# Block 2's half rows by mirrored gathers and scatters instead of TensorE flips, with a new issue order

## The chip, the cores and the metric

The kernel runs on one core of a Trainium2 chip. The metric is the device time of one execution in microseconds (us). Each engine takes its instructions in the order in which the program issues them: PE (TensorE), DVE (VectorE), ACT (ScalarE), POOL (GpSimd), and SP, which here only issues DMAs. Lines such as L617 are lines of the kernel's source.

## The reference

The inputs are `q`, `k`, `v` (2048 rows S of 640 columns D, bf16), a short filter `shift_k` (640 x 4), a long filter `ssm_k` (640 x 2048), a vector `ssm_D`, and three matrices of a SwiGLU feed-forward network (FFN) with 1728 inner columns. Cut to what matters, the reference computes:

```
k_shift[t] = sum over i = 0..3 of k[t-i] * shift_k[:, i]      (causal, per column)
kv  = k_shift * v
y   = causal convolution of kv with ssm_k along the 2048 rows (by FFT) + kv * ssm_D
h   = q + layernorm(q) * y
g   = layernorm(h)
out = h + (silu(g @ w_gate) * (g @ w_up)) @ w_down
```

## The kernel before

**Blocks and tiles.** The 2048 rows are four blocks n = 0..3 of 512; a block is four tiles q = 0..3 of 128 rows, one row to a partition. The long convolution is done by blocks: every block of `kv` and of the filter is taken to a spectrum of 512 values with constant matrices (`WX` for the rows, `WG` for the filter, `WI` back), spectra are multiplied and added over pairs of blocks, and the sum is taken back.

**Half rows and their mirror images.** The basis is symmetric, so the way back needs half of the work: `inverse` (L587) makes, for each half m = 0, 1, an even part `es` and an odd part `os`, 128 rows each (PE L597, copied from PSUM by ACT L601). Their sum is rows of tile 2+m in natural order; their difference is rows of tile 1-m in mirrored order (last row first). Tiles 0 and 1 of a block thus come out mirrored. The letter of the block in `HOW` (L101) says what is done about it:

- `J`: the block's rows are loaded in natural order by one DMA of SP (L274). The difference is turned by PE: four matmuls with the flip matrix (L617) of `es` and `os` into a PSUM buffer of pool A, which DVE multiplies by the normalized rows (L620). Then DVE adds each tile to its rows (L610 and L622).
- `G`: SP loads tiles 2 and 3 only. Tiles 0 and 1 are fetched mirrored, by two indirect DMAs of POOL (`load_x`, L577) with a constant table of row numbers (`mirror`). DVE forms the difference with L608, as it forms the sum, and handles the natural and the mirrored tile together by L626 (multiply) and L627 (add), 128 x 1280 each. The two tiles stay mirrored through the FFN, row by row, and their results are written back by indirect DMAs of POOL (`down`, L752), where `J` uses a plain store of SP.

With `HOW = 'GGJJ'`, blocks 0 and 1 go by gathers and scatters, blocks 2 and 3 by flips:

```python
if half == 0 or HOW[n] != "J":
    add("DVE", ..., (TA, TS)[half](y[:, 1 - half, :], es[m][:], os_[m][:]))       # L608
else:
    nc.tensor.matmul(ps(g)[:, h, 0:NH], flip[part], (es, os_)[part][m][...], ...)  # L617
    add("DVE", ..., TM(r3(y[:, 1 - half, :]), ps(g)[:, :, 0:NH], r3(xln[...])))    # L620
```

**The other stages.** `g_transform` (L344 on PE, L346 on ACT) makes a filter block's spectrum from the transposed filter: block 0's is transposed by PE (L314), blocks 1 to 3 by a transposing DMA of SP (L304). `front` makes `kv` of a block: for block 0 DVE multiplies rows with the short filter (L383) and PE shifts and adds them (L393), turning tiles 0 and 1 (V: L401, ACT L403, DVE L404/L406); for later blocks DVE does all of it (L361, L366, L367, L368) and PE turns two tiles (L418). L421 and L422 fold the block into its even and odd halves. `x_transform` is L433 on PE and L438 on ACT. `pair` is DVE's spectral products and sums (L443, 128 x 2560). `ln` takes sums over rows on ACT (L527, L530, L531), `root` the inverse square root on POOL (L550), `scale` the normalized rows on DVE (L563) or ACT (L559, L560). SP transposes normalized rows for the FFN (L648). `ffn` is L685 on PE (two groups of five matmuls for each of 14 column chunks, U), `sg` (L690) and `uc` (L697) on ACT, and their product `tT` (L699) on DVE; then the down projection on PE (L733 adds the residual, L736), `o` on ACT (L745) or DVE (L747), and the store. The last tile ends with L714 and L719.

**Openings for POOL.** `port` (L537) is a small DVE reduction (128 x 96) that a POOL instruction is made to wait for. Every scatter (L752) and most roots (L550) have one; the gathers (L577) have none. For some roots a one-column DVE copy of the result follows (L552).

**Buffers.** PSUM has two pools of two buffers, A (transforms, inverses, flips) and F (filter transforms, FFN). `es`, `os`, `hl`, `sg`, `uc`, `ot`, `wg`, `wu`, `k4`, `vt`, the rows `x` and the transposed rows `hT` have two buffers each. Block 2's rows use the buffer of block 0's, so they can be fetched once block 0's down projection has read them.

**The order.** All instructions are first collected in a list of 1017 entries (`Plan.add`), an entry being some matmuls of one PSUM group, one DVE instruction, one DMA and so on. They are then issued in the order of `SEQUENCE` (L105), a constant permutation of the entries' numbers; nothing else orders them, beyond the waits for data and buffers that each one carries:

```python
def order(self):
    assert sorted(SEQUENCE) == list(range(len(self.ops)))
...
with tc.manual_schedule():
    for i in seq:
        plan.ops[i]["fn"]()
```

Of the kernel before, what the change touches and what calls it, by code (L numbers as in the profile page):

```python
# [97 lines left out]
VEC = (0,)  # L98
SPAN = 96
TURN = ()  # L100
HOW = 'GGJJ'  # L101
BACK = "SSSS"
TRANS = {1: 0, 2: 0, 3: 0}
WARM = (0.43, 5, 0)
SEQUENCE = [int(i) for i in """  # L105
2 19 20 5 0 8 10 7 1 3 24 21 22 34 72 69 4 11 13 12 14 17 15 73 16 25 18 27 26 28 6 31 61 71 29 23 30 56 53 54 51 62 32 76 33 74 229 58 63 52 77 64 57
75 55 78 65 206 59 198 80 60 207 228 79 35 89 66 199 70 43 67 36 81 68 37 208 90 38 98 91 82 209 39 99 85 83 210 44 92 86 40 100 230 93 88 233 45 101
234 94 200 102 46 41 95 103 96 201 42 47 97 202 104 106 48 148 105 203 49 211 149 214 109 221 150 315 50 220 116 314 108 156 215 151 204 157 107 172
205 158 173 111 212 159 190 216 213 174 231 110 118 114 191 222 175 112 115 152 217 113 223 160 153 218 237 117 132 224 119 219 130 133 225 434 120
327 161 164 326 226 131 433 121 442 182 165 441 227 176 183 137 123 134 184 177 135 122 248 136 192 249 138 185 256 124 139 193 250 257 166 125 140  # L110
186 141 167 251 194 128 187 126 129 142 443 154 195 232 127 162 87 143 435 155 252 235 196 180 163 253 258 146 168 197 436 147 259 444 254 238 144 178
181 145 169 260 179 170 245 261 255 188 171 243 236 262 316 437 263 242 189 317 9 438 321 244 318 322 338 319 246 323 439 339 333 324 320 239 247 328
334 325 330 350 445 335 264 329 336 345 265 331 351 449 340 332 266 341 342 362 346 446 343 337 268 347 352 363 348 344 353 267 357 349 269 358 359
354 272 355 270 375 360 401 440 369 402 374 240 271 455 370 361 274 429 371 273 364 372 356 275 430 365 278 387 386 276 277 293 399 279 456 373 366
450 451 295 367 388 398 381 400 296 280 452 382 299 281 294 447 394 457 383 384 297 376 368 385 431 395 377 396 284 453 389 300 378 432 379 390 285
380 403 458 391 392 298 404 448 397 301 282 405 393 283 302 459 406 305 478 410 306 286 411 460 407 477 303 412 304 454 408 413 287 461 423 291 307
409 462 289 292 475 489 414 497 424 290 84 308 498 476 490 499 559 415 491 677 479 500 417 312 416 481 501 313 310 418 480 492 311 419 483 560 420 571
493 421 572 425 482 494 502 426 484 495 463 503 561 485 504 427 562 496 487 563 566 564 486 567 568 583 565 578 569 584 505 669 464 579 570 488 580
573 581 574 507 575 465 590 596 506 595 576 591 468 577 469 509 585 466 586 607 582 510 467 513 608 428 592 508 536 593 514 602 587 594 511 588 470
603 471 589 597 512 537 598 604 472 671 599 515 600 620 619 605 288 473 679 614 670 516 422 521 678 522 712 517 615 606 538 523 616 617 518 609 544  # L120
601 519 672 539 610 631 611 520 632 711 626 525 633 612 627 526 618 613 680 621 628 524 629 713 622 540 623 634 541 527 681 715 635 624 528 639 625
673 636 630 545 637 682 640 529 692 542 650 641 546 691 530 814 543 651 547 548 642 638 549 652 674 714 685 686 532 653 675 550 717 643 533 551 693
644 813 654 801 802 534 645 552 694 535 646 655 553 695 657 716 647 676 658 555 687 556 683 663 648 656 684 688 557 696 664 689 554 649 690 558 474
697 665 698 659 719 733 741 718 734 666 735 667 720 660 736 803 699 742 721 661 804 805 737 723 806 808 738 722 809 810 825 743 725 811 826 739 700
815 701 807 812 727 816 817 820 818 724 744 821 702 837 819 726 822 832 838 823 703 833 824 728 706 827 740 729 828 834 849 835 731 829 745 850 830
844 704 831 845 836 746 749 705 839 730 846 840 847 861 841 751 851 842 862 707 747 843 856 848 748 732 853 852 873 708 874 750 857 662 854 858 863
241 709 752 859 868 753 869 860 754 757 870 761 864 755 758 871 779 910 765 875 756 881 780 855 759 872 865 309 866 781 760 867 531 882 762 766 883
763 876 782 884 764 783 877 784 769 785 788 770 786 922 710 891 767 668 878 768 879 892 773 787 775 880 893 771 776 789 772 885 790 909 791 894 774
792 886 777 778 895 887 795 793 921 797 794 888 798 903 889 796 904 890 799 896 800 897 898 899 900 905 901 906 916 907 917 918 911 919 920 912 913
933 908 923 914 934 915 924 925 928 926 927 929 930 945 935 931 946 932 936 937 940 938 939 941 942 957 952 943 958 902 944 953 954 947 955 956 948  # L130
949 969 964 950 970 951 959 960 961 982 981 965 962 966 976 967 983 968 977 963 978 989 979 980 971 990 991 972 973 984 974 975 985 992 986 993 987
988 994 995 996 999 997 1000 998 1001 1002 1005 1003 1006 1004 1007 1008 1011 1009 1014 1012 1013 1010 1015 1016
""".split()]


def dve(n, psum=False):
    return (120 + n) / 960 if psum else 0.06 + n / 1920
# [7 lines left out]
def kernel(  # L145
# [107 lines left out]
    def r3(a):  # L253
        return a.rearrange("p (a b) -> p a b", a=2)

    def ps(group):
        return ps_of[group[0]][plan.held[group]]
# [241 lines left out]
    def ln(n, q, which, pr, t0=0.0):  # L499
# [12 lines left out]
        else:  # L512
            j = q % 2
            if which == 1 and HOW[n] == "X" and q < 2:
                g = ("A", "M", n, q)
# [38 lines left out]
    def scale(dst, n, q, which, key, pr):  # L554
        s, src, c = sm[n, q, which], xin[n % 2][:, q, :], column(n, q, which)
        vec, r = which == 2 and n in VEC, rstd[:, c:c + 1]

        def on_act():
            nc.scalar.activation(s[:, 2:3], s[:, 0:1], ACT.Copy, scale=r)  # L559
            nc.scalar.activation(dst, src, ACT.Identity, scale=r, bias=s[:, 2:3])  # L560

        def on_dve():
            nc.vector.tensor_scalar(dst, src, s[:, 0:1], r, op0=ALU.subtract if vec else ALU.add, op1=ALU.mult)  # L563
        on = (n, which) in XACT and not vec
        add(*(("ACT", act(D) + 0.22, on_act) if on else ("DVE", 0.355, on_dve)), r=[f"sm{n}{q}{which}", f"x{n % 2}_{q}"], w=[key], pr=pr)
# [5 lines left out]
    @stage  # L571
    def load_x(n, pr, queue="SP"):
        if HOW[n] == "G":
            x = xin[n % 2]
            load(queue, x[:, 2:4, :], xq[n * MB + 256:(n + 1) * MB, :].rearrange("(m p) d -> p m d", p=P), [f"x{n % 2}_{q}" for q in (2, 3)], pr, 320, t0=(14, 30, 0, 0)[n])
            for q in (1, 0):
                add("POOL", 2.5, lambda q=q: nc.gpsimd.indirect_dma_start(out=x[:, q, :], out_offset=None, in_=xq[:, :], in_offset=mirror(n, q), bounds_check=S_TOT - 1,  # L577
                                                                      oob_is_err=False), r=["idx"], w=[f"x{n % 2}_{q}"], pr=pr, kb=160, t0=(14, 30, 0, 0)[n])
        else:
            load(queue, xin[n % 2][:], xq[n * MB:(n + 1) * MB, :].rearrange("(m p) d -> p m d", p=P), [f"x{n % 2}_{q}" for q in range(4)], pr, 640, t0=(14, 30, 0, 0)[n])  # L580
        for q in range(4):
            ln(n, q, 1, pr + 30, t0=(26, 50, 0, 0)[n])
        for qs in ((2, 1), (3, 0)) if n == 0 else ((0, 1, 2, 3),):
            root(n, qs, 1, pr + 30)

    @stage
    def inverse(n, pr):  # L587
        a, ak = A[n], Ak[n]
        x, b = xin[n % 2], n % 2
        for m in range(2):  # L590
# [13 lines left out]
            for half, q in pairs:  # L604
                yk, lk, xk = keys[q]
                scale(xln[:, 1 - half, :], n, q, 1, lk, pr)
                if half == 0 or HOW[n] != "J":
                    add("DVE", dve(D), lambda m=m, half=half: (TA, TS)[half](y[:, 1 - half, :], es[m][:], os_[m][:]), r=[f"eo0{m}", f"eo1{m}"], w=[yk], pr=pr)  # L608
                    if HOW[n] == "J":
                        add("DVE", dve(D), lambda half=half: TM(y[:, 1 - half, :], y[:, 1 - half, :], xln[:, 1 - half, :]), r=[lk], w=[yk], pr=pr)  # L610
                else:
# [8 lines left out]
                    add("DVE", dve(D, True), lambda g=g, half=half: TM(r3(y[:, 1 - half, :]), ps(g)[:, :, 0:NH], r3(xln[:, 1 - half, :])), r=[g, lk], w=[yk], pr=pr, rel=("A", g))  # L620
                if HOW[n] == "J":
                    add("DVE", dve(D), lambda q=q, half=half: TA(x[:, q, :], x[:, q, :], y[:, 1 - half, :]), r=[yk], w=[xk], pr=pr)  # L622
            if HOW[n] != "J":
                lo, step = 1 - m, 1 + 2 * m
# [213 lines left out]
```

## Time and profile before

| | us |
|---|---|
| median of 6 runs (lowest, highest) | 285.39 (284.8, 286.09) |
| the profiled execution | 285.3 |
| its span, from first to last instruction | 283.5 |
| PE busy | 272.9 (96%) |
| DVE busy | 218.4 (77%) |
| ACT busy | 207.4 (73%) |
| POOL busy | 36.1 (13%) |

The granted TensorE clock is 1.000. The slices of the profile cut the span in 40 parts of 7.09 us; a digit is the busy share of a slice in tenths, 9 being 90% or more. A line of the chain or the timeline gives the start, the duration, the engine and the source line; in the timeline `out<-in` follows, then the shape, how many instructions were put together (x4), and in brackets how long the engine was idle before and what ended that. SPq is the DMA-issuing queue of SP. Durations on POOL are rough.

### The profile page before, as it was taken

To read this page: it belongs to the slowest core of one execution; us is meant where nothing else is said; L and a number is where in the kernel's file an instruction comes from. 1 tells how busy PE (TensorE), PEld (TensorE's weight loads), DVE (VectorE), ACT (ScalarE), POOL (GpSimd) and SP (SyncE) were. 2 spreads that over 40 slices of the span, in tenths; PEclk is the share of its full clock that TensorE was granted. 3 is DMA by queue.
4 is the path that set the end of the run, shared out by engine and by line. 5 is a ranking of instruction groups with operands and counts; after the bars stand their busy time and mean duration, and the time that the engine had idled before them with its cause. 6 is when DMAs were issued, how large, how long until landed. Compare 5 with 4: busy or idle time off the path is not lost.

```text
span 283.5 us, 4423 instructions
## 1 busy us (share of the span) xinstructions
PE 272.9 (96%) x1639; PEld 160.6 (57%) x1639; DVE 218.4 (77%) x295; ACT 207.4 (73%) x408; POOL 36.1 (13%) x30
## 2 busy tenths in 40 slices
PE   6699999999999999989999999999999999999995
PEld 1467777776444547654455477644455765444673
DVE  1659999999999999999999999999997510211212
ACT  4698898899654999956999997689859945546300
POOL 3203000111800005600030102100300110000000
PEclk9999999999999999999999999999999999999999
DMA  5999991822475870499837099535522561664011
GB/s 169 327 293 319 201 315 27 299 49 46 103 233 136 263 252 1 104 221 250 247 93 205 20 295 217 139 95 152 139 57 71 140 144 29 200 165 116 0 49 46
DMA packets 69466, 44.13 MB, mean 156 GB/s; under 512 B 28290, under 2 KB 67267, under 8 KB 69316
## 3 DMA queue, kind: packets, MB, share of 16 engines
q1 hardware_dynamic: 68914, 42.33, 55.7%
q0 software_dynamic: 384, 1.31, 1.4%
q8 instruction: 13, 0.21, 0.3%
q10 hardware_dynamic: 146, 0.20, 0.2%
q14 instruction: 9, 0.07, 0.1%
HBM read 36.63 MB, written 2.62 MB: 138 GB/s over the span
## 4 chain that ended last, share of the span: by engine, by line
DVE 35%; PE 26%; ACT 8%; issue 3%; DMA 2%; DVEq 0%; ACTq 0%
DVE s L443 14%; PE psF L685 14%; PE psF L736 9%; DVE T L443 9%; DVE tT L699 3%; DMA hT<-hl 2%; DVE k L361 2%; ACT junk L530 2%; PE psF L714 1%; ACT junk L527 1%; ACT sg L690 1%; ACT uc L697 1%; DVE k L366 1%; DVE k L367 1%; PE psA L597 1%
## 5 line engine op out<-in xcount | busy, mean ns | idle before, releaser
L685 PE MATMUL psF<-hT,wg 128*128 128x512 bf16 x280 | 68.7, 379 | 1.7 <-DMA hT<-hl 1.0
L685 PE MATMUL psF<-hT,wu 128*128 128x512 bf16 x260 | 64.0, 379 | 0.0
L736 PE MATMUL psF<-wd,tT 128*128 128x320 bf16 x420 | 60.0, 299 | 0.0
L736 PEld LDWEIGHTS <-tT 128*128 128x128 bf16 x420 | 41.1, 98 | 16.1
L690 ACT ACTIVATE sg<-psF 128x512 bf16<-128x512 f32 (+1 forms) x56 | 33.1, 595 | 21.1 <-DVE tT L699 12.0
L550 POOL TENSOR_TENSOR rstd<-var,mhalf 128x2 f32<-128x2 f32 (+2 forms) x15 | 25.2, 1681 | 178.2 <-ACT var L531 146.4
L699 DVE TENSOR_TENSOR tT<-sg,uc 128x512 bf16<-128x512 bf16 (+1 forms) x56 | 22.9, 420 | 31.7 <-ACT uc L697 31.6
L443 DVE TENSOR_TENSOR s<-s,T 128x2560 bf16<-128x2560 bf16 x32 | 47.0, 1484 | 0.1
L443 DVE TENSOR_TENSOR T<-s,s 128x2560 bf16<-128x2560 bf16 x32 | 46.9, 1484 | 0.0
L685 PEld LDWEIGHTS <-wg 128*128 128x128 bf16 x280 | 27.2, 98 | 32.8 <-issue 3.0
L685 PEld LDWEIGHTS <-wu 128*128 128x128 bf16 x260 | 25.3, 98 | 30.5 <-DMA wu<-in_B_w_up_dram 0.6
L697 ACT CAST uc<-psF 128x512 bf16<-128x512 f32 (+1 forms) x56 | 32.4, 586 | 9.6 <-PE psF L685 9.5
L344 PEld LDWEIGHTS <-s 128*128 128x128 bf16 x256 | 25.0, 98 | 10.1 <-issue 0.3
L344 PE MATMUL psF<-wd,s 128*128 128x320 bf16 x192 | 28.7, 299 | 0.1
L346 ACT CAST s<-psF 128x640 bf16<-128x640 f32 x32 | 21.6, 693 | 4.8 <-PE psF L344 4.5
L530 ACT ACTIVATE junk<-x,sm 128x640 uint8<-128x640 bf16 x28 | 23.3, 833 | 0.5
L438 ACT CAST s<-psA 128x640 bf16<-128x640 f32 x29 | 19.6, 697 | 3.4 <-PE psA L433 3.4
L433 PE MATMUL psA<-kv,WX 128*128 128x320 bf16 x128 | 21.2, 299 | 0.4 <-ACT s L438 0.3
L443 DVE TENSOR_TENSOR s<-s,s 128x2560 bf16<-128x2560 bf16 x14 | 20.8, 1484 | 0.2
L527 ACT ACTIVATE junk<-x 128x640 uint8<-128x640 bf16 x28 | 20.6, 738 | 0.3 <-DVE x L622 0.3
L597 PE MATMUL psA<-s,WI 128*128 128x320 bf16 x128 | 19.2, 299 | 0.6 <-DVE s L443 0.5
L361 DVE TENSOR_TENSOR k<-k,w 128x2560 bf16<-128x2560 bf16 x12 | 17.8, 1485 | 0.5 <-DMA k<-in_A_k_dram 0.5
(78 smaller groups left out, 257.4 us busy)
## 6 DMA issues: line engine op xcount, KB each, us to landing
k<-in_A_k_dram SPq DMA_DIRECT2D x12, 640.0 KB, 6.2
wu<-in_B_w_up_dram SPq DMA_DIRECT2D x24, 320.0 KB, 3.8
wg<-in_B_w_gate_dram SPq DMA_DIRECT2D x24, 320.0 KB, 3.6
v<-in_A_v_dram SPq DMA_DIRECT2D x12, 160.0 KB, 5.6
wd<-in_B_w_down_dram SPq DMA_DIRECT2D x3, 640.0 KB, 6.7
out_dram<-o SPq DMA_DIRECT2D x11, 160.0 KB, 3.5
x<-in_A_q_dram SPq DMA_DIRECT2D x2, 640.0 KB, 5.4
s<-const_wg SPq DMA_DIRECT2D x1, 1024.0 KB
```

The costliest lines, as they stand in the source:

```text
L344: nc.tensor.matmul(ps(g)[:, h, 0:NH], WG[:, kt, ct * P:(ct + 1) * P], gT[p][:, kt, h * NH:(h + 1) * NH], start=(kt == 0), stop=(kt == 3))
L361: add("DVE", dve(4 * D), lambda: nc.vector.tensor_mul(kd[:], kd[:], w4[:]), r=["w4"] + ks, w=[kn], pr=pr)
L443: add("DVE", dve(n * D), lambda: f(o, a, b), r=ks(ak) + ks(bk), w=ks(ok), after=["WG0", "WG1"] if ok[:2] == "s7" else [], pr=pr)
L527: add("ACT", 0.74, lambda: nc.scalar.activation(junks[j][:], src, ACT.Copy, scale=-1.0 / D, accum_out=s[:, 0:1]), r=[xk], w=[k + "a", f"ju ...
L530: nc.scalar.activation(junks[j][:], src, ACT.Square, bias=s[:, 0:1], accum_out=s[:, 1:2])
L550: add("POOL", 0.8, lambda: nc.gpsimd.tensor_tensor(rstd[:, c0:c1], var[:, c0:c1], mhalf[:, 0:c1 - c0], op=ALU.pow), r=deps + gkey + ["mhal ...
L597: nc.tensor.matmul(ps(g)[:, h, 0:NH], WI[:, 4 * part + ct, m * P:(m + 1) * P], a[part][:, ct, h * NH:(h + 1) * NH], start=(ct == 0), stop= ...
L685: i = nc.tensor.matmul(ps(gr)[:, which, :], w[:, kt, cc * P:(cc + 1) * P], hT[b][:, kt, :], start=(kt == 0), stop=(kt == 4))
L690: apart(gr, 0, nc.scalar.activation(sg[s][:z, :], ps(gr)[:z, 0, :], ACT.Silu))
L697: add("ACT", act(MB), lambda gr=gr, s=s, z=z, merged=merged: nc.scalar.copy(uc[s][:z, :], ps(gr)[64:128, 0, :] if merged else ps(gr)[:, 1, ...
L699: add("DVE", dve(MB), lambda c=c, s=s, z=z: TM(tT[:z, c * MB:(c + 1) * MB], sg[s][:z, :], uc[s][:z, :]), r=[f"sg{s}", f"uc{s}"], w=[f"tT{c ...
L736: nc.tensor.matmul(ps(gr)[:, h, 0:NH], tT[:, c * MB + m * P:c * MB + (m + 1) * P], wd[:, c, h * NH:(h + 1) * NH], start=(c == 0 and not re ...
```

## The change

`HOW` becomes `'GGGJ'`: block 2's tiles 0 and 1 are gathered mirrored, kept mirrored and scattered back, and PE flips only block 3's. No function's text changes; `load_x`, `inverse` and `ffn` take their other branch for n = 2. As other entries are added for that block, the entries' numbers shift, and `SEQUENCE` is a new permutation of again 1017 entries; it differs in all stages, not in block 2's alone.

```diff
-HOW = 'GGJJ'
+HOW = 'GGGJ'
...
 SEQUENCE = [int(i) for i in """
-2 19 20 5 0 8 10 7 1 3 24 21 22 34 72 69 4 11 13 12 14 17 15 73 16 25 18 27 26 28 6 31 61 71 29 23 30 56 53 54 51 62 32 76 33 74 229 58 63 52 77 64 57
...
+2 19 10 7 0 8 20 5 1 3 24 21 22 71 34 4 11 72 199 13 207 12 23 14 15 17 16 73 18 25 27 26 28 29 31 51 30 32 56 52 53 61 58 54 57 59 55 230 74 64 76 62
...
```

Decoded for the places that the text comes to:

```
SP, first loads
-  idx, D, filter 0, k, v, WX, filter 1 (transposing), x0 tiles 2-3, WG, k4 1.1, k4 1.0, v 1.1, x1 tiles 2-3, WI, v 1.0, filter 2, filter 3
+  D, idx, filter 0, k, v, x0 tiles 2-3, WX, v 1.0, v 1.1, WG, k4 1.1, k4 1.0, filter 1, filter 2, WI, k4 1.2, v 1.2, k4 1.3, filter 3
DVE, block 0's products by the short filter (L383)
-  tiles 2, 1, 0, and 3 after a kv product
+  tiles 0, 1, 2, then rev of tile 0 (L404), 3
PE, block 0's front
-  V0, S2, V1, S0, S1, S3, first filter transform
+  S0, V0, V1, S1, S2, S3, first filter transform
POOL, between the root of block 1's first half and that of block 2
-  scatter of block 0, root of block 1's second half, scatter of block 0
+  root of block 1's second half, scatter and scatter of block 0, gather and gather of block 2
PE, end of the last inverse (block 3)
-  L597, flip of half 0, ten L685 of FFN 2's chunk 12, flip of half 1
+  ten L685 of FFN 2's chunk 12, L597, flip of half 0, L733 and L736 of a tile, flip of half 1
```

(k4 1.2 is the k tile 2 of block 1 for the short filter; S and V are the shift convolution and the turned v tile of block 0.)

## The prediction

> **What bounds the kernel now.** I read the page's busy table and forty slices first, then the chain that ended last, then the timeline at the places where the chain changes engine. The profiled execution took 285.3 us, span 283.5, so 1.8 us lie outside the span; the median of the six runs is 285.39, and 0.3% (0.86 us) is about what a measurement of this kernel can tell from no change. All durations below are from that one execution, and the sum goes from its 285.3.
>
> ```profile
> PE 272.9 (96%) x1639; PEld 160.6 (57%) x1639; DVE 218.4 (77%) x295; ACT 207.4 (73%) x408; POOL 36.1 (13%) x30
> PE   6699999999999999989999999999999999999995
> DVE  1659999999999999999999999999997510211212
> DVE 35%; PE 26%; ACT 8%; issue 3%; DMA 2%; DVEq 0%; ACTq 0%
> ```
>
> PE is full from the third slice to the last but one, and DVE is full too from the fourth slice to the thirtieth. So two engines bind side by side up to 214 us, and from there PE alone. The end of the chain shows the handover:
>
> ```profile
> 212.31 1.50 DVE s L443
> 213.82 0.04 issue
> 213.86 2.33 PE psA L597 x16
> 216.19 0.54 PE psA L617 x4
> 216.74 2.16 PE psF L685 x10
> ...
> 265.18 11.41 PE psF L736 x84
> 276.59 3.82 PE psF L714 x28
> 280.43 0.49 DVE o L719
> ```
>
> The last spectral product of block 3 ends on DVE at 213.82; PE starts the last inverse at once and then has work without a break to 280.43. Two sums thus set the end: all PE work, with its gaps, and DVE work up to that product plus the PE work ordered behind it. In the windows view PE is busy 79.22 of 20 to 100, 111.71 of 100 to 214 and 66.40 of 214 to 281: under 3.1 us of gaps from 20 to 280.4. What moves the end is PE work, the date of PE's start, and those gaps.
>
> **Part 1: block 2's flips leave PE.** Rows of one L617 group are at 149.24, 149.38, 149.51 and 149.65, the other group at 161.91 to 162.32: a matmul starts each 0.136 us, so a group costs 0.54, as the chain's row at 216.19 says for block 3. Two groups: **-1.09 us of PE**, all on the path, as PE is 99% busy there. Block 3 keeps its flips.
>
> **Part 2: DVE.** Start to start, a half block m pays now L610 0.40, L620 from PSUM 0.73 (150.77 to 151.50) and two L622 0.80: 1.93. It will pay one more L608 0.40, L626 0.73 and L627 0.74, as block 0's rows at 106.83 and 107.90 do: 1.87. Two halves save 0.12. Two scatters bring two L537 openings of 0.16 (75.75 to 75.91), but after 230 us, where DVE is busy 18.27 of 67: nothing on the path. Before 214 us DVE gains 0.12; I count 0.
>
> **Part 3: POOL and SP.** SP issues 320 KB for block 2's rows instead of 640, and two gathers of 160 KB go to POOL, behind block 0's two scatters; two of block 2's stores go from SP to POOL, near 235 us, 45 us before the end: nothing. The gathers are the open cost. Existing ones took 1.01 to 2.00 us of POOL and landed 6.1 to 7.2 us after issue; scatters landed after 2.7 to 5.5.
>
> ```profile
> 4.78 1.01 POOL L577 DMA_INDIRECT x<-in_A_q_dram,idx  x1 [0.31 <-issue]
> 12.39 2.00 POOL L577 DMA_INDIRECT x<-in_A_q_dram,idx  x1 [6.49 <-DVE k L383]
> 117.08 1.43 POOL L752 DMA_INDIRECT out_dram<-o,idx  x1 [0.37 <-ACT o L745]
> 176.91 1.23 POOL L752 DMA_INDIRECT out_dram<-o,idx  x1 [5.21 <-DMA out_dram<-o,idx]
> ```
>
> In the new order POOL runs: root 1 of block 1's second half, scatter of tile 1, scatter of tile 0, gather, gather, root of block 2. I place block 0's scatters about as now, 113.6 and 117.1; the second may wait for the first to land, as the 5.21 shows. With 1.4 for the scatter and 2 for each gather, the gathers are issued by 121 to 123 and land by 128 to 130. ACT's first statistics of these rows (L527) stand now at 132.57; I place them near 130, for the new order is earlier there. So they fit, without much room: 0 is taken, 4.4 the far end (last rival).
>
> One rule is weighed here. The row at 12.39 ran beside two back-to-back L383 products with both inputs in SBUF and took 2.00 against 1.01 with DVE idle; the row at 176.91 ran beside L421 and L422, which also read two SBUF tiles, and took 1.23. The Trainium skill's page "SBUF — State Buffer", section "Who interferes with whom", says that a DVE instruction with two SBUF inputs contends with a GpSimd instruction that reads SBUF, yet infers that descriptor generation needs only the write side, which such products leave free. By the inference each gather would cost its idle 1.01 and the forecast would stand; by the first half each would wait for a product to end, at worst for a hole in DVE's stream, which is the last rival.
>
> **Part 4: the start is reordered.** This is the largest term, and nothing in it is about flips.
>
> ```profile
> 3.93 9.41 SPq L304 DMA_TRANSPOSE wd<-in_A_ssm_k_dram  x1
> 9.23 1.49 DVE L383 TENSOR_TENSOR s<-x,w 128x2560 bf16<-128x2560 bf16 x1 [5.06 <-DMA x<-in_A_k_dram]
> 14.00 0.47 SPq L274 DMA_DIRECT2D s<-const_wg  x1
> 18.85 2.06 PE L393 MATMUL psA<-s,perm 128*128 128x320 bf16 x14
> 20.75 3.10 PEld L344 LDWEIGHTS <-s 128*128 128x128 bf16 x24 [0.17 <-DMA s<-const_wg]
> 20.75 3.43 PE L344 MATMUL psF<-wd,s 128*128 128x320 bf16 x24
> ```
>
> Now SP spends 3.93 to 13.34 on the transposing load of filter block 1, so WG, PE's first large operand, is issued at 14.00 and arrives at 20.75, when PE has just ended the last shift convolution. DVE multiplies tile 2 first, then 1, 0, 3, with other work between, so PE waits for products. In the new order SP issues k, v, block 0's rows, WX, two small v tiles and WG, then two k tiles, and only then filters 1 and 2; DVE multiplies tiles 0, 1, 2 in a row, and PE convolves 0, 1, 2, 3. Keeping 9.23 for the first product and 1.40 a product, and PE groups of 1.09 (8 matmuls) or 1.9 (14), PE's convolutions run 10.75 to 11.85, 12.6 to 14.5, 14.5 to 16.4 and 16.5 to 18.45. WG must be there by then. Up to WG some 4.9 MB are issued; the slices moved 169, 327 and 293 GB/s in their 7.09 us each, thus 3.5 MB by 14.2 and the rest by 18.9. PE's first filter matmul comes at 18.45 to 18.9 instead of 20.75: **-1.9 to -2.3 us**. On DVE the front of block 0 (L422, ends at 23.50 now) moves to about 20.8 by the same products, which lets the DVE chain go **-2.4**. The filters' transposes, issued later, land near 26 and 30 by their 6.7 to 9.4 us of SP time each, against uses at about 30 and 32; cover of 2 to 4 us, and if it is gone the PE gap is at most what Part 4 gave.
>
> **Part 5: the middle and the last third.** One gap of PE can go:
>
> ```profile
> 127.57 1.24 PE L685 MATMUL psF<-hT,wg 128*128 128x512 bf16 x5 [0.99 <-DMA hT<-hl]
> ```
>
> Block 1's FFN waits there for a transposed tile; the new order has it some 4 us before PE needs it: 0 to -0.99. Against that I see three tight places (block 1's first inverse behind its product, a flip of block 2's front, the start of FFN 0), each 0.25 to 0.6 by the distance of the two instructions in the two orders: 0 to +1.1. I let the two cancel. Before block 3's last product, DVE gets two tT products more (0.34 each, start to start at 209.14; together about +0.6 with the rest of the moves), and PE gets ten L685 (2.16, the row at 216.74) ahead of the last inverse instead of behind it. DVE's way to the end: -2.4 + 0.6 - 2.16 = -4.0. PE's way: -1.09 - 2.1 = -3.2. The later one decides: PE.
>
> **Sum.** 285.3 - 3.2 = 282.1; I add 0.2 for waits that a new order brings and that no row of the old trace can show: **282.3**, a span of 280.5. Its own range is 280.9 (the gap at 127.57 gone and nothing new) to 283.8 (all tight places, WG at 18.9, 0.5 more).
>
> **Rivals.**
> *Only the flips count.* WG or the k tiles behind it come no earlier, as the DMA engines are 90% busy in the first 20 us by the windows view, and the late filters give back the rest. Then -1.09 remains: 284.2. For it: the start is a queue of bytes as much as of instructions. Against it: 9.41 us of SP before WG is a row, not a guess. Chance 0.2, its sizes spread from 283.5 to 285.
>
> *The gathers come late: slower.* The place is FFN 1. Block 2's gathers have no L537 opening of their own, as every scatter has, and follow two scatters of which the second may wait for the first. Around 117 to 130 DVE runs L443 products almost without a hole. If a gather gets through only at the first holes now seen, before the tT products at 130.55 to 137.56 (up to 0.33 us each), it is issued near 128 and lands at 134 to 135, while ACT's L527 stands in order near 130, ahead of the next sg and uc. Behind it wait uc, then DVE's tT, then both F buffers and with them PE: +4.4, or +6 if both gathers miss. 282.1 + 4.4 = 286.5, up to 288. It decides once the gathers cost over 3.2 us, that is, land later than about 133. For it: 2.00 beside L383, and root rows beside such products (6.55 at 70.14), although those also contain the wait for their own opening. Against: 1.23 at 176.91. With this goes any other stall of that size in the new order. Chance 0.3, from 285 to 288.
>
> *Nothing changes in substance*, as DVE binds and not PE: excluded up to 214 us by Part 5, where DVE's own way is shorter than PE's by 0.8; it is held in the first rival's spread.
>
> **How the numbers follow.** Forecast 0.5, flips only 0.2, late gathers 0.3. Within 0.3% of 285.39 means 284.53 to 286.25. The forecast is faster throughout (0.50); of the flips-only case 0.13 is faster and 0.07 the same; of the late gathers 0.04 is the same and 0.26 slower. Faster 0.63, same 0.11, slower 0.26. The range leaves out about 0.1 at each side: 280.9 to 286.8.
>
> **What would show it.** Right: the first L344 at 18.4 to 18.9; eight L617 instead of sixteen; no PE gap before FFN 1; gathers of 1 to 2 us near 118 to 123 and L527 of these rows without a wait; the last L443 ending near 211.5, with some 64 us of PE behind it. Wrong: a first L344 still past 20; a hole of 3 us or more on ACT, DVE and PE between 125 and 140 that ends on the gathers' DMA; PE waits for filters at 26 to 33; or PE gaps from 20 to 280 that add up to well over the 3.1 us of now.

## The result, and the profile after

The changed kernel is faster, by about half of what was forecast: a median of 284.37 us (21 runs, 283.02 to 285.35) beside 285.88 of the kernel before (47 runs, 284.8 to 287.89); the ratio is 0.994, with a 95% interval of 0.9925 to 0.9955, that is 1.3 to 2.1 us. The forecast was 282.3.

The two profiled executions say less than the medians: 285.19 with a span of 283.1 after, 285.3 with 283.5 before. Only one of the changed kernel's 21 runs was slower than its profiled one. The page's busy line and the line on the chain of waits, of the changed kernel:

```profile
PE 272.8 (96%) x1631; PEld 160.6 (57%) x1631; DVE 218.6 (77%) x295; ACT 207.8 (73%) x408; POOL 38.6 (14%) x34
...
PE 27%; DVE 9%; ACT 6%; issue 2%; ACTq 0%
```

DVE's share of the chain reads 35% before and 9% after, but the two chains are not of one length: the old one is followed back to 70.48, the new one only to 157.77. From 157.77 on, the pieces of the old chain add up to 56 us of DVE and 67 of PE, those of the new one to 25 of DVE, 16 of ACT and 77 of PE. The new chain runs mostly along ACT to 172.7, along DVE to 199.3, and along PE from 202.2, with 3.5 us of ACT ahead of the last inverse. PE has the eight flips less (1631 for 1639), and its rows for L617 in the groups view are 4 and 4 instead of 8 and 8. The first piece of the chain, and its end (start, duration, engine, buffer, line):

```profile
157.77 0.56 ACT uc L697
...
215.03 0.59 ACT es L601
...
215.66 2.33 PE psA L597 x16
...
276.02 3.82 PE psF L714 x28
...
279.86 0.49 DVE o L719
```

The end is 0.57 earlier than before, but the start is later. PE's part of the timeline, first of the kernel before, then of the changed one (start, duration, line, shapes, how many matmuls):

```profile
12.36 1.27 PE L393 MATMUL psA<-s,perm 128*128 128x320 bf16 x4
13.43 1.01 PE L393 MATMUL psA<-k,perm 128*128 128x320 bf16 x3
...
15.86 3.15 PE L393 MATMUL psA<-k,perm 128*128 128x320 bf16 x22
```

```profile
11.20 2.29 PE L393 MATMUL psA<-k,perm 128*128 128x320 bf16 x8 [1.15 <-DVE k L383]
...
14.35 3.42 PE L393 MATMUL psA<-k,perm 128*128 128x320 bf16 x14
...
19.51 2.06 PE L393 MATMUL psA<-s,perm 128*128 128x320 bf16 x14
21.41 3.42 PE L344 MATMUL psF<-wd,s 128*128 128x320 bf16 x24
```

The first filter matmul comes at 21.41, later than the old 20.75, although PE's first convolution starts at 11.20 and PE then never waits. The reason stands in the counts. From 11.20, eight matmuls and then four take until 14.35: one each 0.27 us. From 19.51, fourteen take 1.9: one each 0.136. Taken row by row, the changed kernel's L393 and L401 start 0.27 apart to 17.0 and 0.136 from there; the old kernel's do so to 15.0. PE runs at half rate at first, and the step to full rate came 2 us later in this execution. The windows view has a granted clock of 1.00 from 10 to 20 us; only the spacing tells.

It is useful to split the time at the first L344. From there to the end of the last L719 is called the body here. In seven of eight profiles with the changed order behind the start, it takes the same time to 0.4 us, wherever the start ends:

| run | first L344 | end of L719 | between | profiled time |
|---|---|---|---|---|
| before | 20.75 | 280.92 | 260.17 | 285.3 |
| changed | 21.41 | 280.35 | 258.94 | 285.19 |
| changed, again (e12) | 19.74 | 278.60 | 258.86 | 283.37 |
| e4, old start | 21.45 | 280.38 | 258.93 | 285.12 |
| e1, PE kept busy | 18.50 | 277.61 | 259.11 | 282.53 |
| e5, late start | 25.93 | 284.81 | 258.88 | 289.54 |
| e6, late start, busy | 23.78 | 283.03 | 259.25 | 287.86 |
| e8, PE kept busier | 18.70 | 277.86 | 259.16 | 282.62 |
| e11, WG first | 18.95 | 279.41 | 260.46 | 284.35 |
| e2, old order, PE kept busy | 21.79 | 281.11 | 259.32 | 285.56 |

So in these seven the time is the first L344 plus 263.6 to 264.1 (e11: 265.4), and the prediction splits into two questions: what the body gave (1.23 us between the profiles of before and after, but 0.38 beside e2, which has the old body too), and what became of the start.

### The profile page after: what moved, and what is told of

Its sections match the earlier page's. It is cut to its first block, busy times and chain, and to the rows that moved or that the text cites. A ratio compares the mean times of both kernels' runs of the same rounds, so it can differ in the third digit from the quotient of the medians.

```text
span 283.1 us, 4406 instructions
## 1 busy us (share of the span) xinstructions
PE 272.8 (96%) x1631; PEld 160.6 (57%) x1631; DVE 218.6 (77%) x295; ACT 207.8 (73%) x408; POOL 38.6 (14%) x34
## 5 line engine op out<-in xcount | busy, mean ns | idle before, releaser
L736 PEld LDWEIGHTS <-tT 128*128 128x128 bf16 x420 | 41.1, 98 | 16.1
L443 DVE TENSOR_TENSOR T<-s,s 128x2560 bf16<-128x2560 bf16 x32 | 47.1, 1484 | 0.1
L443 DVE TENSOR_TENSOR s<-s,T 128x2560 bf16<-128x2560 bf16 x32 | 46.9, 1485 | 0.1
L550 POOL TENSOR_TENSOR rstd<-var,mhalf 128x2 f32<-128x2 f32 (+2 forms) x15 | 21.0, 1403 | 177.0 <-ACT var L531 147.5
L344 PEld LDWEIGHTS <-s 128*128 128x128 bf16 x256 | 25.0, 98 | 10.3 <-issue 0.3
L344 PE MATMUL psF<-wd,s 128*128 128x320 bf16 x192 | 28.6, 299 | 0.1
L433 PE MATMUL psA<-kv,WX 128*128 128x320 bf16 x128 | 21.3, 299 | 1.0 <-DVE kv L422 0.7
L527 ACT ACTIVATE junk<-x 128x640 uint8<-128x640 bf16 x28 | 20.7, 740 | 0.0
L443 DVE TENSOR_TENSOR s<-s,s 128x2560 bf16<-128x2560 bf16 x14 | 20.7, 1482 | 0.0
L361 DVE TENSOR_TENSOR k<-k,w 128x2560 bf16<-128x2560 bf16 x12 | 17.6, 1482 | 0.0
```

The lines of the kernel that those rows point to most:

```text
L344: nc.tensor.matmul(ps(g)[:, h, 0:NH], WG[:, kt, ct * P:(ct + 1) * P], gT[p][:, kt, h * NH:(h + 1) * NH], start=(kt == 0), stop=(kt == 3))
L433: nc.tensor.matmul(ps(g)[:, h, 0:NH], WX[:, kt, ct * P:(ct + 1) * P], kv[:, base + kt, h * NH:(h + 1) * NH], start=(kt == 0), stop=(kt == 1))
L443: add("DVE", dve(n * D), lambda: f(o, a, b), r=ks(ak) + ks(bk), w=ks(ok), after=["WG0", "WG1"] if ok[:2] == "s7" else [], pr=pr)
L527: add("ACT", 0.74, lambda: nc.scalar.activation(junks[j][:], src, ACT.Copy, scale=-1.0 / D, accum_out=s[:, 0:1]), r=[xk], w=[k + "a", f"ju ...
L736: nc.tensor.matmul(ps(gr)[:, h, 0:NH], tT[:, c * MB + m * P:c * MB + (m + 1) * P], wd[:, c, h * NH:(h + 1) * NH], start=(c == 0 and not re ...
```

## The experiments

Theory A was that PE's half rate sets the new start, theory B that DVE's products or a DMA do. A time is a median with the lowest and highest execution in brackets; ratios are to the kernel before on the same chip.

**e1, e2: PE kept busy before the front.** Dummy matmuls of constants fill PE's early holes.

```diff
+ before the first L314:  3 matmuls ident x perm, 320 columns, into the buffer that L314 then overwrites
+ before the first L393:  5 of them (e1, on the changed kernel)
+ before the first L401:  7 of them (e2, on the kernel before)
```

> The changed kernel with eight dummy 128x320 matmuls of constants in PE's early holes (three before the first L314, five before the first L393), nothing else. Theory A (in the start PE runs at half rate, 0.27 us a matmul instead of 0.136, until a step that comes only after PE has been busy for some time, and the new start is bound by that): the step comes before 11.5, no L393 is 0.27 from the next, the first L344 comes at 18.6 to 19.4 instead of 21.41, and the time is 282.3 to 283.2 against 284.4 of the changed kernel. Theory B (the start is bound by DVE's products or by WG's arrival): the first L344 stays past 20.7 and the time at 284.4 within 0.5.

> The kernel before with ten dummy matmuls (three before the first L314, seven before the first L401). Theory A: PE reaches the step earlier here too, but WG arrives at about 20.6 in the old order, so the first L344 stays at 20.6 to 20.8 and the time gains 0 to 0.7 against 285.9, the upper part only from executions in which the step came late. Theory B: no change, 285.9.

e1: 283.76 (282.53 to 284.91), ratio 0.9943 (0.9921 to 0.9964). PE's timeline in its profiled execution:

```profile
10.04 1.14 PE L389 MATMUL psA<-perm 128*128 128x320 bf16 x5
11.02 1.25 PE L393 MATMUL psA<-k,perm 128*128 128x320 bf16 x8
...
18.50 3.42 PE L344 MATMUL psF<-wd,s 128*128 128x320 bf16 x24
```

L389 are the dummies. The step falls among them, the eight L393 take 1.1 instead of 2.1, and the first L344 comes at 18.50, 2.9 earlier than in the changed kernel's profile; the end is 2.74 earlier. Theory B would have it past 20.7. The traffic of the DMA engines does not make the half rate: their busy share is 1.05 from 10 to 12 us and 1.08 from 12 to 14 here, 1.05 and 1.07 in the changed kernel. But the profiled execution is the fastest of the seven. The median, 283.76, missed its 282.3 to 283.2, and the ratio is no better than the changed kernel's: see e8.

e2: 285.75 (284.9 to 287.87), ratio 1.0007 (0.9987 to 1.0027): no gain. Here the dummies sit behind a buffer that ACT frees only at 11.0, so PE idled from 10.25 to 11.03 all the same, and the half rate lasted to 16.1. The run shows something else: its first L344 is 1.04 later than in the profile of before, and its end 0.19. The delay passes through the transforms and is taken up at FFN 1:

```profile
126.72 1.25 PE L433 MATMUL psA<-kv,WX 128*128 128x320 bf16 x8
127.81 1.24 PE L685 MATMUL psF<-hT,wg 128*128 128x512 bf16 x4
```

In the profile of before these rows start at 125.33 and 127.57: the first is 1.39 late, the second 0.24, as the wait of 0.99 for the transposed rows is gone. The old body is held there by a DMA, so an earlier start of the old order is worth little; the changed body waits 0.23 there.

**e5, e6: the price of the half rate by itself.** DVE's first product is done four times, so that the convolution starts 4.7 to 5.0 us later; e6 adds dummies that keep PE busy until then.

```diff
-add("DVE", ..., lambda: nc.vector.tensor_mul(prod, kfirst[...], w4[:]))            # L383
+add("DVE", ..., lambda: [nc.vector.tensor_mul(...) for _ in range(4 if q == 0 else 1)])
+ e6 only: 3 dummies before the first L314, 26 before the first L393
```

> The changed kernel with DVE's first product (L383 of tile 0) done four times, so that PE's first L393 comes 4.2 us later, near 15.4; PE idles from 10 to there. Theory A (half rate until a step 3.4 to 6.8 us after PE's last idle stretch, at a moment that differs from execution to execution): L393 0.27 apart at first, first L344 at 24.6 to 26.3, time 288.4 to 290, spread of its executions over 1.2. Theory B (DVE's products or DMAs set the start): first L344 near 23 whatever PE's rate, 286.8.

> The same late start with 3 and 26 dummy matmuls before it (before the first L314 and the first L393), so that PE is busy from 6.7 to past 13.5 and the step must be past in every execution when L393 begins. Theory A: every L393 0.136 apart, first L344 near 22.9, time 286.4 to 287.1, 1.7 to 3 us under the late start without dummies, and the spread of its executions shrinks to 0.7 or less. Theory B: as the late start without dummies.

PE's timeline of e5, then of e6:

```profile
15.94 2.29 PE L393 MATMUL psA<-k,perm 128*128 128x320 bf16 x8 [5.64 <-DVE k L383]
...
19.09 3.20 PE L393 MATMUL psA<-k,perm 128*128 128x320 bf16 x14
...
25.93 1.25 PE L344 MATMUL psF<-wd,s 128*128 128x320 bf16 x8
```

```profile
10.12 4.04 PE L389 MATMUL psA<-perm 128*128 128x320 bf16 x26
16.21 1.25 PE L393 MATMUL psA<-k,perm 128*128 128x320 bf16 x8 [2.06 <-DVE k L383]
...
23.78 3.42 PE L344 MATMUL psF<-wd,s 128*128 128x320 bf16 x24
```

From the first L393 to the first L344 e5 takes 9.99 and e6 7.57, with the same work and the same waits for DVE. The medians are 289.47 (287.51 to 290.08) and 286.48 (285.88 to 287.86): 2.99 us for nothing but PE having been busy. That is theory A. The spread was to shrink to 0.7: it is 2.0 in e6, ten of twelve executions within 0.94. In the profiled execution, the longest of e6, the L393 start 0.136 apart, so what is left there is not the step. A candidate is the k load: DVE's first product starts when it has landed, between 8.89 and 10.09 in the fourteen profiles, and 10.09 is e6's.

**e4, e3: the start and the body taken apart.** The first 120 entries of one order stand before the rest of the other.

```diff
e4 = changed kernel: + 120 first entries of the old SEQUENCE, then the others in the new order
e3 = kernel before:  + 120 first entries of the new SEQUENCE, then the others in the old order
```

> The changed kernel with the first 120 entries of the old order put first and the rest as changed: the flips gone, the start as it was. Theory A: the flips' 1.1 us of PE are gone and the start is worth 0 to 0.5: 284.4 to 284.9 against 285.9 of before. If the flips gave nothing and all of the gain is the start (rival): 285.9.

> The kernel before, flips of block 2 kept, with the first 120 entries of the new order put first and the rest as before. Theory A: first L344 at 20 to 21.5, as the step falls, and a time of 285.0 to 285.9. If the start gave what the prediction's Part 4 said (rival): first L344 at 18.5 to 18.9 and about 283.8.

e4: 285.0 (284.01 to 286.16), ratio 0.9984 (0.9967 to 1.0002), 0.5 to 0.6 better than before with an interval that just takes in no change, and a little short of what was expected; the changed kernel has 0.994. By the ratios the new start is thus worth 1.3 and the rest of the change 0.5 (interval -0.1 to 0.9); by the medians of the times (285.88, 285.0, 284.37), not all from one chip, 0.6 and 0.9.

e3: 288.55 (288.52 to 291.82), ratio 1.0123. It does not measure the start: behind the mixed order PE waits 2.03 us at 41.6 for block 3's filter, which SP issues too late there. Two by-products are worth keeping. Four of its six executions lie within 0.04 us (288.52 to 288.56), as they would if a DMA at a fixed time took up whatever the start did; all executions of the other kernels spread over 1.6 to 4.2 us. And in the profiled execution, 290.67 and not one of the four, the granted clock falls after that hole (last section).

**e7, e9, e10: the flips alone, both ways.**

```diff
e7, e9 = new order, HOW = 'GGJJ':  L608 -> L617; L626 -> L620, L610; L627 -> L622, L622
         gathers and scatters -> plain load and stores
         e7: whole load where the half load stands;  e9: where the second gather stood
e10    = old order, HOW = 'GGGJ':  the reverse; both gathers right behind block 0's second scatter
```

> The changed order with block 2's flips, plain load and plain stores put back (HOW as before, the entries in their places). If PE's work sets the end in the changed order, the flips' 1.09 us come back whole: 285.3 to 285.7 against 284.4. If holes of PE take them up (rival): 284.4 to 284.7.

> Block 2's flips back in the changed order as in e7, but with the whole load of block 2's rows at the place of the second gather, so that it is not late. From the first L344 to the last L719 the changed order takes 258.9 in every run so far. If the flips' 1.09 us of PE are all on the path: 260.0, and a time of 285.3 to 285.7 against 284.4. If holes of PE take them up: 258.9 to 259.3 and 284.4 to 284.7.

> The old order with HOW = 'GGGJ': each entry that goes is dropped, the new ones stand in the same places, the two gathers right behind block 0's second scatter. From first L344 to L719 the old order took 260.2 and 259.3 in two runs. If the flips are on the path there too: 258.3 to 259.1, time 284.8 against 285.9. If the old order is held by something else near 125 to 137 us, where a start that was 1.0 later had been made up: 259.3 to 260.2, time 285.5 to 286. If the gathers come late without places chosen for them (the prediction's last rival): over 287.

e7: 288.61 (286.44 to 289.69), ratio 1.0076. Its load is late, PE has a hole of 2.27 us at 135.2, and the granted clock falls after it; so it says little on the flips. e9: 286.9 (285.18 to 288.58), ratio 1.0043 (1.0018 to 1.0069), over the 285.3 to 285.7 that were expected. Its body takes 262.79, 3.85 more than the changed one. 1.70 of that is gone by block 1's fold, before any instruction that differs, and has another cause, DVE waiting for block 1's k tile:

```profile
24.60 1.49 DVE L361 TENSOR_TENSOR k<-k,w 128x2560 bf16<-128x2560 bf16 x1 [2.12 <-DMA k<-in_A_k_dram]
```

This load was issued at 18.03 in e9 and in e12, the changed kernel, and landed at 24.58 and 22.69: executions differ there. The other 2.15 lie behind that fold. FFN 1 starts 1.2 late (a PE wait of 1.36 behind a scatter that landed late, next to the larger load). The two groups of flips then add 0.54 and 0.55, but 0.55 is gone again at block 3's first transform, where PE waits for DVE. The row of the changed kernel, then of e9:

```profile
174.43 0.70 PE L433 MATMUL psA<-kv,WX 128*128 128x320 bf16 x4 [0.71 <-DVE kv L422]
```

```profile
176.18 0.70 PE L433 MATMUL psA<-kv,WX 128*128 128x320 bf16 x4 [0.16 <-DVE kv L422]
```

The last 0.4 comes behind the last inverse, 0.25 of it in a wait for weights. So the flips' 1.09 of PE come back, but half of it stands where the changed kernel waits anyway: in this order they are worth 0.54 on the path, close to the 0.5 of e4.

e10 is the surprise: 288.45 (287.01 to 291.18), ratio 1.01 (1.0048 to 1.0152). The flips away, without the order made for it, is slower than before. It is not that POOL is kept from gathering: the two gathers ran at 119.82 and 121.39, beside L443 products, in 1.26 and 1.17 us. They landed 7.4 to 7.5 us after issue, where the changed kernel's took 3.1. They put 320 KB on the DMA engines ahead of the transposed rows and weights that FFN 1 waits for; no run moved the gathers alone, so this last step is a reading of the order. PE, and the granted clock of three windows of 2 us (start and end, length, busy time and count of PE, PEld, DVE, ACT and POOL, clock, DMA share, GB/s):

```profile
129.65 0.46 PE L685 MATMUL psF<-hT,wg 128*128 128x512 bf16 x1 [2.08 <-DMA hT<-hl]
```

```profile
128.00:130.00 2.00, 0.35 (x1) 0.22 (x3) 2.00 (x2) 1.49 (x3) 0.00 (x0) 0.95 1.15 279
130.00:132.00 2.00, 1.78 (x5) 0.67 (x5) 1.50 (x2) 0.14 (x1) 0.00 (x0) 0.50 1.20 290
132.00:134.00 2.00, 2.00 (x8) 0.82 (x7) 0.00 (x0) 0.76 (x2) 0.00 (x0) 0.69 0.54 166
```

The wait for the transposed rows grew from 0.99 to 2.08, and PE then lost another 1.72 us to the clock in this execution. Three of the five executions have a mean granted clock of 0.999 or more and still took 287.0 to 288.5. In this order, what the change took off PE gave nothing.

**e8, e11, e12: a better version?**

```diff
e8  = e1 + one dummy after the second L314 group, 6 instead of 5 before the first L393
e11 = e8, with WG's load issued right behind k and v
e12 = the changed kernel
```

> The changed kernel with one more dummy in the hole between the first two pairs of L314 and six instead of five before the first L393, against the kernel with eight dummies. Theory A: the step cannot come after 13.4, first L344 18.5 to 19.7, time 282.4 to 283.6, so 0.5 to 1.5 under the changed kernel's 284.4. Theory B: 284.4.

> The kernel of e8 with WG's load issued right behind k and v, ahead of block 0's rows, WX and two v tiles. Five of e8's ten executions lie near 284.5, five at 282.0 to 283.5. If WG's late arrival makes the slow ones: all executions at 282.0 to 283.3. If the step or the arrival of k makes them: as e8, median 283.9, spread over 2.

> The changed kernel itself, for a comparison with e11 on one chip: 284.4, executions from 283.0 to 285.4; first L344 between 19.2 and 21.6, that is the time less 263.8, with 0.27 between the first L393.

e8: 283.88 (282.05 to 284.94), ratio 0.9922 (0.9892 to 0.9953). e11: 283.57 (282.74 to 284.35), ratio 0.9921 (0.9893 to 0.9949). e12: 283.88 (282.82 to 284.96), ratio 0.9943 (0.992 to 0.9966). All three beat the kernel before; they are not told apart from one another or from the 0.994 of the change. The lowest execution of all, 282.05, is e8's. But e8's median missed its 282.4 to 283.6, and e11's lies between its two cases and decides for neither. Why half of e8's executions stay near 284.5 is open. A candidate is block 1's k tile, which is issued only when the products have left its buffer. DVE's wait for it at L361 was 2.12 in e9 (above), 0.23 in e12 and 1.21 in e11, whose first L344 came at 18.95 but whose body took 260.46; e8's own profile, at 282.62, has no such wait.

e12 shows the same program in another execution:

```profile
10.84 2.29 PE L393 MATMUL psA<-k,perm 128*128 128x320 bf16 x8 [0.85 <-DVE k L383]
...
13.99 2.11 PE L393 MATMUL psA<-k,perm 128*128 128x320 bf16 x14
```

The fourteen matmuls of tile 1 take 1.95 to the next row instead of 3.26, because the step came at 14.2 and not at 17.2; the first L344 is 1.67 earlier and the time 1.82 lower (283.37 and 285.19).

## Why the prediction was right or wrong

- **What bounds the kernel**: right for the old kernel in that two engines bind, incomplete in that its body is also held by a DMA at FFN 1 (e2). In the new order PE alone was to set the end, with DVE's last product done at 211.5 (the prediction's own terms, 213.82 - 2.4 + 0.6, give 212.0). It ends at 215.51, 0.1 us before the ACT copy (L601) that releases the last inverse at 215.66. So PE, idle for 0.34 there, has the most work, but ACT and DVE are right behind it, and the chain runs mostly along them from 157.77 to 202.2.
- **Part 1, flips, -1.09, and Part 5, waits that cancel, with +0.2**: right as a sum for the two profiles, where the body gained 1.23; wrong in that all of the 1.09 is on the path. PE's windows from 20 us on have 3.2 us of gaps, 3.1 before: the 0.99 at FFN 1 went (0.23 is left), others came (0.79 between 80 and 100, 0.71 between 160 and 180, 0.64 between 200 and 220). The 0.71 is the wait for DVE that takes up half of the flips' time (e9). Beside e2's old body the gain is 0.38, by e4's ratio 0.5. e10 says that even this holds only with an order made for it.
- **Part 2, DVE, nothing**: right as to work, 218.6 busy beside 218.4.
- **Part 3, gathers, nothing, and the rival of late gathers**: right for the reason given, wrong in the rival's mechanism. In the changed kernel:

```profile
126.52 1.19 POOL L577 DMA_INDIRECT x<-in_A_q_dram,idx  x1 [0.30 <-issue]
128.01 1.17 POOL L577 DMA_INDIRECT x<-in_A_q_dram,idx  x1 [0.31 <-issue]
```

They are 5 us later than I placed them, as the second scatter started only at 124.05. But they landed 3.1 us after issue and not 6 to 7, at 129.66 and 131.15, so L527 of the rows, at 131.49, comes without harm, with 0.3 us of room. Beside L443 products they take 1.2, not the 2.00 of the start. These products read two SBUF tiles, so the inference of the Trainium skill's page "SBUF — State Buffer", section "Who interferes with whom", that descriptor generation is not held up by them, agrees with 1.17 to 1.26 here; no gather waited for a hole in DVE's stream. The rival's sign was possible all the same: e10 is slower, by way of the DMA engines if the reading given there holds.
- **Part 4, the start, -1.9 to -2.3**: this is the step that failed. It measured +0.66 in the profiled pair, -1.01 in e12's execution, and 0.6 to 1.3 of gain by e4's comparison. The order of the entries worked as described: products in a row, convolutions 0, 1, 2, 3, WG early (e1's first L344, at 18.50, waits for nothing). The term was mis-sized by the duration: 1.09 for 8 matmuls and 1.9 for 14 are full-rate durations, taken from the row at 18.85, while four matmuls from 12.36 to 13.43 of the same trace take 1.07. From the first L393 at 11.20 there are 54 matmuls (the sum left out the four L401, but had holes for them); at 0.136 each they end at 18.54. Each of the 21 slow ones cost 0.13 more, together 2.8, which makes 21.3. With PE kept busy (e1) the first L344 came at 18.50 and the profiled time at 282.53; that the medians of e1 and e8 gain less is not explained.

The step itself is what the Trainium skill's page "TensorE: Matmul & The Clock Gate" describes in Part 1, "The HAM clock gate": PE is at half rate until it has been busy through a whole window of about 3.4 us, and the windows run freely, so the step moves from execution to execution. The runs agree: PE's first matmul after its idle stretch of 0.67 us or more and the last slow one lie 2.6 to 5.8 us apart in ten profiles (11.86 to 15.0 before, 11.20 to 17.0 after, 10.84 to 14.0 in e12); 2.6, in e9, is less than a window of 3.4, so by that length a window counts before it is busy throughout. The earlier L327 and L314 did not bring the step, with holes between them and 0.67 us or more idle after. An estimate made afterwards: with some 3 to 6 us of half rate from the first convolution, as in the ten profiles, and half of it lost, Part 4 would have been -0.6 to +0.9 and the forecast about 284.5.

## What to carry to other kernels

Look at how far apart equal matmuls start, at the very place whose time is being worked out; a duration from later in the trace holds only if PE has been busy for some microseconds before. Work that was pulled ahead into a PE that had been idle was done at half rate here. Dummy matmuls in the idle stretch gave 2.99 us where the start was made late (e5, e6); on the changed kernel itself they are not told apart from no effect by the medians (e1, e8). Work taken off a busy engine gives its full time only where nothing else waits next: of the flips' 1.09 half was taken up by a wait for another engine. And taking work off one engine by adding DMAs needs a place for those DMAs: the same edit gave 1% more time in one order and belonged to a gain in the other.

## What the runs showed of the hardware

- After holes of 2.03 (e3), 2.27 (e7) and 2.08 us (e10) in a busy PE, the granted clock of the profiled executions fell to 0.50 and was back within three windows of 2 us. The windows add up to 1.70, 1.72 and 1.72 us lost: half of 3.4 each time, as the window of the page named above has it. After holes of 0.99 (before) and 1.36 (e9) it stayed at 1.00. So in these three executions a hole of two microseconds cost nearly four.
- Not every execution pays this. A mean granted clock of 0.994, which is what 1.7 us lost makes of 288, is on record for 2 of 6 executions of e3, 8 of 10 of e7, 2 of 5 of e10 and 3 of 11 of e9 (not its profiled one), and for none of the other kernels. How long the holes were in executions without a profile is not known.
- The half rate at the start is in no clock column of these profiles (1.00 in all windows from 10 to 20 us); the dips after holes are.
- The same program's start ended at 19.74 and at 21.41 in two executions. By its extreme executions the change could have passed for a loss of 0.5 or a gain of over 4; the split at the first L344 is what made the profiles comparable.
